# Attention with beacon keys, then an ELU feed-forward, on one core: batch 2's q and k loaded directly and transposed on TensorE, another order of work

## The chip, the core and the metric

The kernel runs on one NeuronCore of a Trainium2 chip. The core has five engines that run side by side and meet at semaphores: TensorE (PE, with its weight loads shown apart as PEld), VectorE (DVE), ScalarE (ACT), GpSimd (POOL) and SyncE (SP). SP, ACT and POOL issue DMAs. The metric is the device time of one execution in microseconds (us), lower is better.

## What is computed

Inputs and output are float32. B = 8 batches, H = 8 heads, S = 576 positions, 16 beacon keys, D = 64; the feed-forward goes from 512 to 2048 and back.

```
scores = (1/8) * q @ concat(beacon_k, k).T      # 576 x 592 for each batch and head
scores = where(causal, -1e9, scores)            # beacon keys are always seen
a      = softmax(scores);  y = a @ concat(beacon_v, v)
x      = y as [B*S, H*D] = [4608, 512]
h      = x @ w_in                               # [4608, 2048]
g      = where(h > 0, h, exp(min(h, 0)) - 1)    # ELU
out    = g @ w_out                              # [4608, 512]
```

## The kernel before

The program is one long list of words, `run("""...""")` near the end. Each word is a call: `F.2.11` is step F with arguments 2 and 11. The words are issued in that order, and each engine takes its own instructions out of them in the same order, so the list sets the order on PE, ACT, DVE, POOL and SP; an engine waits only for its own data, for the buffers that it writes, and for what is ahead of it in its queue.

*Loads of q and k.* `BD` is the number of batches, counted from 0, that are loaded directly. For these `lq.b.n.h0.h1` (L136, two DMAs, q and k, issued by POOL) casts a segment of rows of heads h0 to h1 to bfloat16 in SBUF (`qst`, `kst`; two buffer sets, batch b uses set b % 2). `T.b.p.n` (L267) turns the pair of heads p by transposing matmuls into PSUM; for b > 0 one T is 24 of them, and its PSUM tile is one of the two buffers with the tag "S", which the scores use too. `ck` (ACT) and `cq` (DVE) (both L280) copy the result to the operand tile `qks[p]`, and `cb.b.p` (DVE, L276) puts the beacon keys of that batch beside it. Batch 0 has two segments of rows, batch 1 one. For the batches from `BD` on, `lk.b.n` (L756, POOL) casts q (n = 0) or k (n = 1) from DRAM to a scratch tensor `scr` in DRAM; `lt.b.x` (L763, SP) reads it back by two DMA transposes, one of `scr` for q and one for k, into `qst` (x = 0, head pairs 0 and 1) or `kst` (x = 1, pairs 2 and 3); `lp.b.x` (POOL) fills in the beacon keys.

*Other loads, all by POOL:* `lv` (v, L144 and L149, one DMA for the beacon rows and one for each chunk of keys), `wi` (w_in, L161, eight DMAs each), `wo` (w_out, L165, one each). POOL keeps eight DMAs under way: an issue waits for the eighth before it to land.

*Attention.* `S.b.i` (L321): scores of a group of columns into an S buffer. `x.b.i` (ACT, L336): exp of it into `et`. `m` (DVE, L341): causal masks. The denominators: for batches below `BD`, `L.b.g` sums over all five chunks of keys by matmuls with ones (L378); from `BD` on, `D.b.p.n` (DVE, L394) adds the chunks up first and L does one matmul per head on the sum (L420). `n` (ACT): its reciprocal, by Ln and Exp. `W` (L378): the product with v. `M` (DVE): scaling into x transposed, `xT`.

*Feed-forward.* Tokens go in tiles t of 512 (tiles 0 and 1 have 256). `F.t.i` (L512): one part of h into a PSUM bank of the tag "hps". ELU has two ways: `e` (ACT, exp), `u` (ACT, relu), `k` (DVE, min of exp - 1 and relu: L537); or `e` (ACT), `r` (DVE, L544: min(exp, 1) - 1), `g` (DVE, L550: max with h). Tiles 8 and 9 have P, K, E, U, V instead of F, e, u, k, a form with seven products in place of eight; U is on ACT, or with `.v` on DVE (L724). `G` and `o`, `s` are the output product of the tiles 0 and 1 and its storing. `wt`, `Z`, `Q`, `J` do the same for the later tiles in the form with seven products; `J` copies or adds a result, on ACT or (`.v`) on DVE. `H` and `X` prepare the sums for P. `Jh.9.0` (copy on ACT, DMA on SP) and `Jh.9.1` (copy on DVE, DMA on ACT; L743, L745) store the last two pieces. `warm` and `wm` are matmuls on zeros whose results nobody reads.

The form of r before, and the step that L takes by batch:

```
nc.vector.scalar_tensor_tensor(
    out=rb[t, i], in0=eb[t, i], scalar=1.0, in1=one32.to_broadcast([P, 512]),
    op0=ALU.min, op1=ALU.subtract)
...
if b >= BD:
    for i in range(4):
        nc.tensor.matmul(
            out=r_[32 * i:32 * (i + 1), QA:S], lhsT=ones,
            rhs=presum[b, 2 * g + i // 2][:, i % 2, QA:S], start=True, stop=True, skip_group_check=True)
else:
    quad(b, g, QA, S, r_[:, QA:S], None, True)
```

Of the kernel before, what the change touches and what calls it, by code (L numbers as in the profile page):

```python
# [17 lines left out]
def kernel(  # L18
# [59 lines left out]
    BD = 2  # L78
# [462 lines left out]
    @step  # L541
    def r(t, i):
        rb[t, i] = melt.tile([P, 512], FP16, tag="r", name="r")
        nc.vector.scalar_tensor_tensor(  # L544
            out=rb[t, i], in0=eb[t, i], scalar=1.0, in1=one32.to_broadcast([P, 512]),
            op0=ALU.min, op1=ALU.subtract)
# [391 lines left out]
```

## Time and profile before

| | |
|---|---|
| median of 3 runs | 339.74 us (339.73 to 340.63) |
| span of the profiled execution | 340.2 us, 8575 instructions |
| mean granted TensorE clock | 0.982 |
| PE's longest wait | 4.39 us, up to 57.04 us |
| PE's last matmul ends | 336.4 us |
| DMA moved | 35.82 MB; 71.9% of 16 engines' span on the queue of POOL, 25.4% on that of SP |

The profile is of one execution on the chip. PE, DVE and ACT are shown with the time that they were busy; an arrow `<-` after an instruction names what ended the idle time before it. Line numbers (L512) are those of the kernel, names like `hps<-xT,w_in` are the tile written and the tiles read. A timeline line gives the start, the time until the last of its instructions ended, engine, line, operation, tiles and count.

### The profile page before, as it was taken

The numbers are of one execution on the slowest core, as the hardware profiler recorded it, in microseconds if no ns is written. First come the engines' busy times: TensorE is split into PE (matmuls) and PEld (weight loads), VectorE is DVE, ScalarE is ACT, GpSimd is POOL, SyncE is SP. The second block draws the span as 40 slices with busy tenths as digits, with TensorE's granted clock in tenths as the row PEclk, the third lists the DMA queues.
The fourth block names the chain that finished last, engine by engine and source line by source line (L and its number), as shares of the span: only waits on it lengthen the run. The fifth ranks groups of instructions, "written<-read, shape, count | busy, mean of one in ns | idle before, by whom it ended". The sixth has DMA issues, their size and how long they took to land. (4 is left out here: it accounts for less than half of the span.)

```text
span 340.2 us, 8575 instructions
## 1 busy us (share of the span) xinstructions
PE 324.1 (95%) x3475; PEld 207.2 (61%) x3475; DVE 286.0 (84%) x603; ACT 280.4 (82%) x458; POOL 90.0 (26%) x117
## 2 busy tenths in 40 slices
PE   6989794999999999999999999999999999999995
PEld 3756562544345566555666655566566788788784
DVE  2764774399989999798999987999899999999872
ACT  2998693879899999999889899979988679977940
POOL 8968626226405094005250050000000000000000
PEclk9998997899999999999999999999999999999998
DMA  9999999999999999979999449100001110020112
GB/s 118 149 179 159 158 178 134 147 162 137 179 158 161 121 141 158 174 145 162 80 145 132 98 26 119 56 31 33 33 31 34 33 63 33 0 94 33 62 65 93
DMA packets 141497, 35.82 MB, mean 105 GB/s; under 512 B 126865, under 2 KB 139921, under 8 KB 141457
## 3 DMA queue, kind: packets, MB, share of 16 engines
q0 software_dynamic: 102592, 18.49, 71.9%
q1 hardware_dynamic: 38144, 16.52, 25.4%
q8 instruction: 27, 0.44, 0.5%
q10 hardware_dynamic: 720, 0.26, 0.3%
q14 instruction: 14, 0.11, 0.1%
HBM read 37.22 MB, written 16.52 MB: 158 GB/s over the span
## 5 line engine op out<-in xcount | busy, mean ns | idle before, releaser
L512 PE MATMUL hps<-xT,w_in 128*128 128x512 f16 (+1 forms) x544 | 120.7, 359 | 1.6 <-DVE gt L550 1.3
L336 ACT ACTIVATE et<-sc 128x1024 f16<-128x1024 f32 (+2 forms) x114 | 105.7, 977 | 9.8 <-PE sc L321 9.5
L623 PEld LDWEIGHTS <-gt 128*128 128x128 f16 x768 | 74.1, 98 | 18.7 <-issue 1.7
L522 ACT ACTIVATE e<-hps 128x512 f32<-128x512 f32 x120 | 73.4, 620 | 13.8 <-PE hps L512 9.2
L512 PEld LDWEIGHTS <-w_in 128*128 128x128 f16 x544 | 50.9, 99 | 45.5 <-issue 8.3
L537 DVE SCALAR_TENSOR_TENSOR gt<-e,r 128x512 f16<-128x512 f32 x108 | 72.5, 684 | 6.1 <-ACT e L522 5.2
L527 ACT ACTIVATE r<-hps 128x512 f16<-128x512 f32 x108 | 65.9, 620 | 3.0 <-PE hps L512 2.9
L623 PE MATMUL ops<-wt,gt 128*128 128x256 f16 x384 | 51.1, 273 | 0.0
L623 PE MATMUL ops<-w_out,gt 128*128 128x256 f16 x384 | 48.9, 273 | 0.0
L149 POOL DMA_DIRECT2D v<-in_v_dram x40 | 35.2, 933 | 17.3 <-DMA scr<-in_k_dram 5.8
L580 DVE TENSOR_TENSOR gt<-gt 128x1024 f16<-128x1024 f16 x48 | 32.3, 685 | 0.3
L341 DVE TENSOR_TENSOR et<-et,triu 128x512 f16<-128x512 f16 (+4 forms) x108 | 31.3, 332 | 1.5 <-ACT et L336 1.5
L394 DVE TENSOR_TENSOR qk<-qk,et 128x672 f16<-128x672 f16 (+2 forms) x72 | 26.0, 370 | 1.0
L378 PEld LDWEIGHTS <-v 128*32 128x32 f16 (+1 forms) x800 | 17.3, 96 | 11.0 <-issue 3.1
L378 PE MATMUL ut<-et,v 128*32 128x464 f16 (+3 forms) x560 | 20.7, 296 | 0.1
L639 DVE TENSOR_TENSOR osb<-ops,sm 128x512 f32<-128x512 f32 x24 | 16.4, 684 | 4.4 <-issue 3.3
L321 PE MATMUL sc<-qst 64*128 64x336 bf16 (+11 forms) x192 | 15.1, 260 | 5.2 <-DMA qst<-scr 4.7
L472 DVE TENSOR_TENSOR xT<-ut,rl 128x672 f16<-128x672 f32 (+12 forms) x26 | 16.5, 671 | 3.2 <-ACT rl L438 1.8
L394 DVE TENSOR_TENSOR qk<-et 128x928 f16<-128x928 f16 x24 | 15.2, 636 | 2.3 <-PE lt L420 1.1
L559 PE MATMUL ops<-w_out,gt 128*128 128x512 f16 x64 | 16.8, 394 | 0.0
L732 DVE SCALAR_TENSOR_TENSOR gt<-e,r 128x512 f16<-128x512 f32 x24 | 15.8, 686 | 1.1 <-ACT e L715 0.8
L623 PE MATMUL ops<-w_out,s 128*128 128x256 f16 x128 | 16.6, 273 | 0.0
(109 smaller groups left out, 383.1 us busy)
## 6 DMA issues: line engine op xcount, KB each, us to landing
out_dram<-osb SPq DMA_DIRECT2D x35, 256.0 KB, 2.3
scr<-in_q_dram POOLq DMA_DIRECT2D x6, 576.0 KB, 14.1
scr<-in_k_dram POOLq DMA_DIRECT2D x6, 576.0 KB, 15.4
v<-in_v_dram POOLq DMA_DIRECT2D x24, 128.0 KB, 7.7
w_in<-in_moe_w_in_dram POOLq DMA_DIRECT2D x16, 128.0 KB, 5.5
w_out<-in_moe_w_out_dram POOLq DMA_DIRECT2D x4, 512.0 KB, 18.1
v<-in_v_dram POOLq DMA_DIRECT2D x8, 112.0 KB, 7.1
v<-in_v_dram POOLq DMA_DIRECT2D x8, 80.0 KB, 8.2
```

Source lines behind the costliest of these rows:

```text
L149: nc.gpsimd.dma_start(out=vt[b][r0:r0 + n, j, :, :], in_=v[b, :, ilo[j]:ilo[j] + n, :].rearrange("h s d -> s h d"),)
L336: nc.scalar.activation(out=ets[b, d][:, :, a - EC2 * d:e - EC2 * d], in_=sc[b, g][:, :, a - c0:e - c0], func=AFT.Exp, bias=0.0, scale=SCALE)
L341: nc.vector.tensor_tensor(out=o, in0=o, in1=i, op=ALU.mult)
L378: nc.tensor.matmul(out=t[32 * i:32 * (i + 1), a - qa:e - qa], lhsT=ones[0:kc[j], :] if half is None else v16[0:kc[j], j, h, 32 * half:32 * ...
L394: (nc.vector if eng == "v" else nc.gpsimd).tensor_tensor(out=o, in0=t[0:rows, :, a:e] if n == 0 else o, in1=t[0:rows, :, col:col + e - a], ...
L512: nc.tensor.matmul(out=h[:, n_, :], lhsT=w_in16[:, cc, P * fc:P * (fc + 1)], rhs=xt[k][:, cc, a - TT * k:e - TT * k], start=(cc == 0), sto ...
L522: nc.scalar.activation(out=eb[t, i], in_=flat(hp[t, i]), func=AFT.Exp, bias=0.0, scale=1.0)
L527: nc.scalar.activation(out=rb[t, i], in_=flat(hp[t, i]), func=AFT.Relu, bias=0.0, scale=1.0)
L537: nc.vector.scalar_tensor_tensor(out=half(t, i), in0=eb[t, i], scalar=1.0, in1=rb[t, i], op0=ALU.subtract, op1=ALU.min)
L559: nc.tensor.matmul(out=ob[t, tb_], lhsT=gt[:, fc, P * tb_:P * (tb_ + 1)], rhs=w_out16[:, fc, :], start=(fc == 0), stop=(fc == NFC - 1))
L580: (nc.vector if eng == "v" else nc.gpsimd).tensor_tensor(out=o_, in0=a_, in1=b_, op=op_)
L623: nc.tensor.matmul(out=xy[t, n_][:, qd, :], lhsT=lw[:, P * qd:P * (qd + 1)], rhs=wt_[:, c, :], start=(first and qd == 0 and c == 0), stop= ...
```

## The change

`BD` becomes 3, so batch 2 takes the way of batches 0 and 1: `lq.2.0.0.4` and `lq.2.0.4.8` in place of `lk.2.*`, `lp.2.*` and `lt.2.*`; four words `T.2`, two `cq.2` and two `ck.2`, four `cb.2`; and no `D.2`, as L sums batch 2 over all chunks on PE. Step r takes another instruction for t of 6 and more. All words are put in another order. In it `wo.0` and `wo.1` stand around batch 2's loads and `wo.2`, `wo.3` behind them, ahead of the casts `lk.3.*`. Twenty parts of h take the way over r and g (twelve before; the six with t of 6 or more use the new r), seven U words are on DVE (four before), and eleven J copies are on DVE (fifteen before, the other four now on ACT). There are 72 `wm` matmuls in place of 59. `Jh.9.1` stands before `Jh.9.0`.

```diff
-    BD = 2
+    BD = 3
...
-        nc.vector.scalar_tensor_tensor(
-            out=rb[t, i], in0=eb[t, i], scalar=1.0, in1=one32.to_broadcast([P, 512]),
-            op0=ALU.min, op1=ALU.subtract)
+        if t < 6:
+            nc.vector.scalar_tensor_tensor(
+                out=rb[t, i], in0=eb[t, i], scalar=1.0, in1=one32.to_broadcast([P, 512]),
+                op0=ALU.min, op1=ALU.subtract)
+        else:
+            nc.vector.tensor_scalar(
+                out=rb[t, i], in0=eb[t, i], scalar1=1.0, scalar2=1.0, op0=ALU.min, op1=ALU.subtract)
...
-    S.1.1 x.1.1 S.1.2 m.0.1.2 H.1.1 x.1.2 lk.2.0 cb.1.2 F.0.2 e.0.2 cb.1.1 S.1.5 x.1.5 F.0.1
-    e.0.1 L.0.B n.0.B lk.2.1 r.0.2 S.1.0 wo.0 g.0.2 r.0.1 g.0.1 F.0.0 wo.1 F.0.3 x.1.0 u.0.3
...
-    x.1.11 e.1.4 r.1.4 S.1.9 wo.2 x.1.6 e.0.6 S.1.7 g.1.4 x.1.7 r.0.6 g.0.6 m.1.0.0 F.1.5 e.1.5
...
-    e.1.2 F.1.0 wo.3 k.1.2 S.1.10 x.1.10 G.0.1.0 G.0.0.0 H.1.2 m.1.1.0 m.1.2.1 m.1.2.0 S.2.3
-    x.2.3 F.0.7 e.0.7 S.2.0 S.2.1 lk.3.0 x.2.1 m.1.3.1 m.1.3.0 x.2.0 G.0.1.1 H.2.2 m.1.0.1 L.1.1
...
+    S.1.8 F.1.5 k.0.4 H.1.0 e.0.6 r.0.6 x.1.8 wo.0 lq.2.0.4.8 g.0.6 G.0.1.0 e.1.5 r.1.5 g.1.5
+    S.1.12 x.1.12 lq.2.0.0.4 wo.1 S.1.9 x.1.9 F.1.2 lv.1.0.1 S.1.10 x.1.10 F.1.3 m.1.2.1 cb.2.1
+    wo.2 e.1.3 T.2.2.0 u.1.3 cq.2.2.0 T.2.1.0 ck.2.1.0 G.0.0.0 e.1.2 u.1.2 T.2.0.0 lv.1.2.3.4
+    ck.2.0.0 lv.2.2.3.4 T.2.3.0 k.1.3 wo.3 cq.2.3.0 F.0.7 G.0.0.1 cb.2.0 e.0.7 m.1.0.0 m.1.2.0
+    S.2.1 x.2.1 wt.1.0 S.2.0 m.1.1.0 G.0.1.1 F.1.0 m.1.0.1 S.2.3 lp.4.0 x.2.0 m.1.1.1 m.2.0.0
+    m.1.3.1 u.0.7 L.1.0 m.1.3.0 e.1.0 r.1.0 g.1.0 x.2.3 F.1.6 n.1.0 M.1.0.0 k.0.7 L.1.1 H.1.2
+    n.1.1 G.0.1.2 lk.3.0 e.1.6 u.1.6 M.1.1.0 lv.2.0.1 k.1.2 W.1.0 M.1.0.1 W.1.1 S.2.2 M.1.1.1
...
-    Q.9.98.105 Q.9.105.112 J.9.5 Jh.9.0 Jh.9.1
+    Q.9.42.49 Q.9.49.56 Q.9.56.63 J.9.2.v Q.9.63.70 Z.9.4.0 J.9.3.v Q.9.70.77 Z.9.4.1 Q.9.77.84
+    Q.9.84.91 J.9.4 Q.9.91.98 Q.9.98.105 J.9.5 Q.9.105.112 Jh.9.1 Jh.9.0
```

More of the change, by code (lines that the diff above doesn't have):

```diff
@@ new lines @@
+    wm.4 x.0.1.1 T.0.2.1 S.0.3.0 wm.4 wm.4 x.0.3.0 T.0.3.1 cq.0.2.1 cq.0.3.1 S.0.2.0 wi.0
+    S.0.2.3 x.0.2.0 wm.4 wm.4 x.0.2.3 wm.4 wm.4 m.0.0.0 m.0.2.0 m.0.1.0 S.0.3.1 x.0.3.1 wm.4
+    S.0.1.2 x.0.1.2 m.0.3.0 cb.1.3 L.0.A S.0.0.3 S.0.2.1 x.0.0.3 x.0.2.1 wm.4 S.0.3.2 x.0.3.2
+    T.1.0.0 n.0.A T.1.1.0 wm.4 wm.4 W.0.A.0 cb.1.0 cq.1.0.0 m.0.2.3 S.1.1 m.0.1.3 m.0.1.2
+    m.0.3.2 cb.1.1 ck.1.1.0 x.1.1 wm.4 wm.4 S.1.2 W.0.A.1 x.1.2 S.0.3.3 x.0.3.3 S.0.2.2 m.0.0.3
+    x.0.2.2 M.0.A.0 M.0.A.1 F.0.2 e.0.2 u.0.2 k.0.2 lv.0.3.4 S.1.5 x.1.5 m.0.2.2 S.1.0 F.0.1
@@ new lines @@
+    m.4.0.1 u.4.3 J.2.6.v S.4.6 S.4.5 Z.3.3.1 m.4.1.0 Q.3.0.7 x.4.5 k.4.3 x.4.6 F.4.7 e.4.7
+    Q.3.7.14 u.4.7 m.4.0.0 F.4.6 S.5.4 e.4.6 u.4.6 m.4.1.1 x.5.4 S.4.7 k.4.8 Q.3.14.21 Z.3.1.1
+    D.4.0.0 Z.3.2.1 J.3.0 lv.5 x.4.7 Q.3.21.28 F.4.9 e.4.9 Z.3.2.0 Q.3.28.35 Z.3.4.0 u.4.9
+    m.4.2.0 k.4.7 k.4.9 S.4.9 x.4.9 S.5.2 x.5.2 F.4.2 D.4.0.1 lk.6.0 J.3.1 e.4.2 r.4.2 F.4.1
+    e.4.1 u.4.1 S.5.3 S.5.0 k.4.6 x.5.0 x.5.3 Q.3.35.42 g.4.2 Q.3.42.49 F.4.5 e.4.5 u.4.5
+    m.4.3.0 D.4.1.0 D.4.1.1 F.4.4 e.4.4 S.4.8 S.5.1 Q.3.49.56 lk.6.1 u.4.4 J.3.2.v lt.6.0
@@ new lines @@
+    D.5.0.0 Q.3.98.105 x.5.12 x.5.7 F.5.6 lp.6.0 S.6.1 e.5.6 k.4.1 x.6.1 lk.7.1 u.5.6 lt.6.1
+    m.5.1.0 Q.4.0.7 Q.3.105.112 Z.4.3.0 D.5.1.0 m.5.1.1 S.6.4 x.6.4 D.5.0.1 S.5.9 x.5.9 k.5.6
+    D.5.0.2 D.5.1.1 J.3.6 k.4.13 Q.4.7.14 F.4.11 e.4.11 u.4.11 F.5.7 Z.4.1.0 Z.4.2.0 S.5.11
+    x.5.11 e.5.7 k.4.11 S.5.8 D.5.1.2 D.5.1.3 lt.7.0 Q.4.14.21 m.5.3.1 x.5.8 F.5.11 e.5.11
+    m.5.2.0 u.5.7 D.5.0.3 Q.4.21.28 W.5.0 J.4.0.v Z.4.1.1 u.5.11 L.5.0 n.5.0 lp.7.0 F.5.14
+    k.5.11 Q.4.28.35 m.5.2.1 F.5.1 Z.4.2.1 H.4.1 D.5.2.0 k.5.7 Q.4.35.42 M.5.0.0 J.4.1 e.5.14
@@ new lines @@
+    x.6.10 S.6.0 F.5.3 Q.4.84.91 k.5.9 F.6.4 x.6.0 e.5.3 k.5.0 D.6.1.0 m.6.0.0 e.6.4 k.5.4
+    D.6.0.0 m.6.0.1 S.6.6 S.6.8 x.6.8 x.6.6 Q.4.91.98 Q.4.98.105 Q.4.105.112 J.4.5 D.6.0.1
+    S.6.11 u.5.3 m.6.2.1 k.5.3 Q.5.0.7 J.4.6.v F.6.11 Q.5.7.14 m.6.1.1 u.6.4 k.6.4 F.6.6 x.6.11
+    S.6.12 e.6.11 r.6.11 S.7.2 Z.5.3.0 Z.5.1.0 Q.5.14.21 e.6.6 g.6.11 Z.5.1.1 u.6.6 x.7.2
+    J.5.0.v Z.5.2.0 Z.5.2.1 D.6.0.2 D.6.1.1 F.6.5 lv.6 x.6.12 F.6.15 e.6.5 u.6.5 S.7.4 x.7.4
+    D.6.0.3 S.6.7 m.6.3.0 Q.5.21.28 Q.5.28.35 e.6.15 D.6.1.2 D.6.1.3 r.6.15 k.6.5 J.5.1 x.6.7
@@ new lines @@
+    Q.6.28.35 m.7.3.1 k.7.10 e.7.13 F.7.1 D.7.1.3 u.7.13 m.7.2.0 D.7.0.3 Z.6.2.1 L.7.0 e.7.1
+    S.7.8 s.1.1 u.7.1 m.7.3.0 D.7.3.0 J.6.1 n.7.0 D.7.3.1 k.7.7 k.7.13 M.7.0.0 Q.6.35.42 H.3.0
+    x.7.8 Z.6.4.1 F.7.4 e.7.4 u.7.4 k.7.4 D.7.2.0 F.7.8 e.7.8 k.7.1 u.7.8 D.7.3.2 m.7.2.1
+    D.7.3.3 k.7.8 Q.6.42.49 Q.6.49.56 F.7.5 e.7.5 u.7.5 Z.6.4.0 H.3.1 F.7.14 e.7.14 D.7.2.1
+    J.6.2 D.7.2.2 Q.6.56.63 r.7.14 F.7.6 e.7.6 u.7.6 Q.6.63.70 J.6.3 Q.6.70.77 k.7.6 F.7.9 W.7.0
+    e.7.9 D.7.2.3 L.7.1 n.7.1 Z.7.3.0 k.7.5 r.7.9 g.7.14 g.7.9 Q.6.77.84 F.7.11 J.6.4 X.8.1
@@ new lines @@
+    E.8.1.6 U.8.1.6 K.8.1.5 J.7.1 Q.7.35.42 E.8.1.5 P.8.2.0 K.8.2.0 Q.7.42.49 J.7.2 P.8.2.1
+    U.8.1.4.v V.8.1.4 Z.7.4.0 K.8.2.1 V.8.1.6 Z.7.4.1 Q.7.49.56 P.8.2.2 K.8.2.2 P.8.2.3
+    Q.7.56.63 X.9.1 K.8.2.3 U.8.2.1 E.8.2.1 U.8.1.5.v P.8.2.4 K.8.2.4 Q.7.63.70 J.7.3 V.8.2.1
+    P.8.2.5 P.8.2.6 V.8.1.5 Q.7.70.77 K.8.2.5 Z.8.3.0 E.8.2.6 Q.7.77.84 J.7.4 F.8.13 Z.8.1.0
+    U.8.2.4 U.8.2.6 V.8.2.6 E.8.2.4 V.8.2.4 M.7.1.1 e.8.13 u.8.13 F.8.15 e.8.15 k.8.13 u.8.15
+    k.8.15 Q.7.84.91 F.8.14 e.8.14 F.8.12 u.8.14 k.8.14 e.8.12 Q.7.91.98 J.7.5 u.8.12 Q.7.98.105
@@ new lines @@
+    k.8.12 P.9.0.0 E.8.2.5 K.9.0.0 U.8.2.5 X.9.2 P.9.0.1 Q.7.105.112 P.9.0.2 K.9.0.1 P.9.0.3
+    E.9.0.1 V.8.2.5 K.9.0.2 Q.8.0.7 X.9.3 Z.8.3.1 K.9.0.3 U.9.0.1 X.9.4 P.9.0.4 K.9.0.4 P.9.0.5
+    K.9.0.5 J.7.6 U.9.0.5 Q.8.7.14 P.9.0.6 E.9.0.6 Q.8.14.21 V.9.0.1 P.9.1.0 Z.8.2.0 U.9.0.6
+    U.9.0.4.v K.9.1.0 Z.8.1.1 E.9.0.4 Q.8.21.28 P.9.1.1 P.9.1.2 J.8.0 Q.8.28.35 Z.8.2.1
+    Q.8.35.42 E.9.0.5 K.9.1.1 P.9.1.3 V.9.0.6 V.9.0.4 K.9.1.2 E.9.1.1 P.9.1.4 J.8.1 V.9.0.5
+    K.9.1.3 K.9.1.4 U.9.1.1 Q.8.42.49 J.8.2 P.9.1.5 Q.8.49.56 E.9.1.4 U.9.1.4 K.9.1.5 U.9.1.5
@@ new lines @@
+    V.9.1.1 V.9.1.4 Z.8.4.1 Z.8.4.0 P.9.1.6 E.9.1.6 U.9.1.6 V.9.1.6 F.9.12 e.9.12 Q.8.56.63
+    u.9.12 Q.8.63.70 k.9.12 E.9.1.5 V.9.1.5 P.9.2.0 K.9.2.0 J.8.3 P.9.2.1 K.9.2.1 E.9.2.1
+    U.9.2.1.v Q.8.70.77 P.9.2.2 K.9.2.2 Q.8.77.84 P.9.2.3 J.8.4 K.9.2.3 Q.8.84.91 V.9.2.1
+    P.9.2.4 Z.9.3.0 Q.8.91.98 K.9.2.4 J.8.5 P.9.2.5 P.9.2.6 K.9.2.5 U.9.2.4 E.9.2.4 Q.9.0.7
+    E.9.2.6 U.9.2.6.v V.9.2.4 V.9.2.6 E.9.2.5 U.9.2.5.v F.9.13 e.9.13 u.9.13 Z.9.1.0 V.9.2.5
+    F.9.14 k.9.13 e.9.14 u.9.14 Q.8.98.105 k.9.14 F.9.15 e.9.15 u.9.15 Z.9.3.1 Q.8.105.112 J.8.6
@@ L909 @@
+    Q.9.7.14 Q.9.14.21 k.9.15 Q.9.21.28 Z.9.2.0 Z.9.1.1 J.9.0 Z.9.2.1 Q.9.28.35 Q.9.35.42 J.9.1
+    Q.9.42.49 Q.9.49.56 Q.9.56.63 J.9.2.v Q.9.63.70 Z.9.4.0 J.9.3.v Q.9.70.77 Z.9.4.1 Q.9.77.84
+    Q.9.84.91 J.9.4 Q.9.91.98 Q.9.98.105 J.9.5 Q.9.105.112 Jh.9.1 Jh.9.0
     """)
```

179 lines of the change are left out of this document (63 added, 116 removed).

## The prediction

> **What bounds the kernel now.** I read the page's busy shares first, then the busy time by windows, then PE's waits, then PE's timeline at the longest of them and the two DMA queues behind it.
>
> ```profile
> PE 324.1 (95%) x3475; PEld 207.2 (61%) x3475; DVE 286.0 (84%) x603; ACT 280.4 (82%) x458; POOL 90.0 (26%) x117
> ```
>
> ```profile
> 24.00:28.00 4.00, 3.71 (x25) 1.80 (x25) 2.71 (x12) 3.22 (x5) 2.35 (x6) 0.57 1.30 158
> ...
> 57.00:62.00 5.00, 4.96 (x24) 1.91 (x24) 1.38 (x2) 3.15 (x4) 1.97 (x3) 0.51 1.72 136
> ...
> 66.00:90.00 24.00, 23.97 (x228) 10.77 (x216) 22.44 (x44) 21.07 (x35) 11.33 (x13) 1.00 2.15 161
> 90.00:140.00 50.00, 49.43 (x532) 27.77 (x532) 47.30 (x105) 47.29 (x76) 17.70 (x17) 1.00 1.78 148
> ```
>
> Columns: the window, its length, busy us and instructions of PE, PEld, DVE, ACT and POOL, the granted clock, DMA share, GB/s. From 66 us PE is busy nearly without a gap to its last matmul at 336.4 us, so whatever PE loses or has to do before or after then comes out at the end one for one. It loses most before 66 us: two stretches at half clock, and these waits:
>
> ```profile
> PE sc L321 <- DMA qst<-scr: 4.7, 2, 4.4
> ...
> PE tp L267 <- DMA kst<-in_k_dram: 1.0, 1, 1.0
> ```
>
> ```profile
> 40.44 0.45 PE L267 MATMUL tp<-identb,qst 96*64 96x96 bf16 x12
> 40.72 0.42 PE L267 MATMUL tp<-identb,kst 96*64 96x96 bf16 x12
> 41.07 0.39 PE L321 MATMUL sc<-hi 64*128 64x400 bf16 x4
> ...
> 57.04 0.61 PE L321 MATMUL sc<-qst 64*128 64x48 bf16 x6 [4.39 <-DMA qst<-scr]
> 57.58 1.89 PE L512 MATMUL hps<-xT,w_in 128*128 128x256 f16 x8
> ...
> 62.09 0.90 PE L378 MATMUL lt<-et,ones 128*32 128x464 f16 x24
> ...
> 62.92 0.89 PE L378 MATMUL lt<-et,ones 128*32 128x464 f16 x24
> ...
> 87.79 0.38 PE L420 MATMUL lt<-qk,ones 128*32 128x464 f16 x4
> ...
> 88.25 1.90 PE L559 MATMUL ops<-w_out,gt 128*128 128x512 f16 x8
> ```
>
> ```profile
> 29.83 2.23 POOL L756 DMA_DIRECT2D scr<-in_q_dram  x1
> 31.53 2.76 POOL L756 DMA_DIRECT2D scr<-in_k_dram  x1
> ```
>
> ```profile
> 41.48 6.97 SPq L763 DMA_TRANSPOSE qst<-scr  x2
> 48.57 8.94 SPq L763 DMA_TRANSPOSE kst<-scr  x2
> ```
>
> This is batch 2's way: POOL issues the casts to DRAM at 29.83 and 31.53, they land at 41.4 and 45.1, SP's transposes start only then, and the second lands at 57.0, where the first scores of batch 2 (S.2.3) start after 4.39 us of nothing. The clock is then 0.51 until 62 us.
>
> **The change, part by part** (against the profiled execution's span of 340.2 us; the runs' median, 339.74, lies 0.46 lower).
>
> (1) *The stall.* Four direct loads of 288 KB replace casts and transposes. Wi.1, the last transfer ahead of both, landed at 33.1. Behind it now come 576 KB of batch 1's q and k, 512 KB of w_out, then 1152 KB for batch 2. The queue's rate: from 33.1 to 45.1 before, 1728 KB landed (144 KB/us); from 45.1 to 78.0, 3792 KB and 1152 KB of transposes (150 KB/us). At 150 the loads are complete at 33.1 + 2240/150 = 48.0 us. PE reaches T.2 by its own work: F.0.2 starts at 24.8 before, and 23 us of PE words (each priced by its row) stand between it and T.2.2.0 in the new order; with the 2 to 3 us of small waits that this stretch has now, 50 us. So the data is ahead and the 4.4 us go: -4.4 (bounds -4.4 and 0).
>
> (2) *The half clock behind it.* F.0.7 took 1.82 us from 57.58 to 59.40, against 0.87 for such a word at full clock, G.0.1.1 1.72 against 0.87, the three score words 0.5 more together: 2.3 us lost. Without the long idle stretch it goes: -2.3. [...]
>
> (3) *New PE work.* Each T.2 is 24 transposes like those at 40.44: 0.63 us to the next word (41.07), four times, 2.5. Batch 2's denominators are summed by PE over all key chunks (L.2 as L.1): 62.09 to 62.92, 0.83 us, in place of 87.79 to 88.25, 0.46; twice 0.37, 0.74. These lie in the bound stretch: +3.3. Thirteen more filler matmuls (some 0.06 us each) stand before 24 us, where ACT is the busy engine (11.3 of 12 us from 8 to 20) and PE would wait for its exponentials: 0, or 0.7 if that cover is gone.
>
> (4) *Drains of T.2.* They are a new link: each T.2 takes one of the two S buffers until a copy of 1.36 us on DVE (two) or 1.10 on ACT (two, rows of batch 1's L280) frees it; queued behind them on ACT are the e and u of F.1.2 and F.1.3, whose banks PE needs. Hidden wholly they cost 0, bare all four 4.9. G.0.0.0 and F.0.7 (0.87 each) lie between and after, and e.1.2 and e.1.3 stand ahead of both ACT copies: nearer to hidden, I take +1.0.
>
> (5) *T.1.3's wait for kst, 0.99 us.* That load took 9.0 us with the two casts behind it; batch 1's first halves took 6.4 and 7.1. At 7 it would land at 36.2, ahead of PE: -0.7 (bounds -1.0 and +1.0).
>
> (6) *DVE and ACT.* They fall out of the bound but not far.
>
> ```profile
> L394 DVE TENSOR_TENSOR qk<-qk,et 128x672 f16<-128x672 f16 (+2 forms) x72 | 26.0, 370 | 1.0
> ...
> L394 DVE TENSOR_TENSOR qk<-et 128x928 f16<-128x928 f16 x24 | 15.2, 636 | 2.3 <-PE lt L420 1.1
> ```
>
> ```profile
> L544 DVE SCALAR_TENSOR_TENSOR r<-e,one 128x512 f16<-128x512 f32 x12 | 8.3, 690 | 6.8 <-ACT e L522 6.6
> ...
> L724 DVE TENSOR_SCALAR r<-kst 128x512 f16<-128x512 f32 x2 | 0.8, 422 | 0.0
> ```
>
> DVE loses batch 2's sixteen presums, (26.0 + 15.2)/6 = 6.9, and four sum copies (2.7); it gains two T.2 copies (2.7), four beacon copies (0.6), one copy of batch 0 (0.8), three U words (1.3), and eight tiles that swap u and k for r and g: 8 x 0.69 for each of r, g and minus k is 5.5, less six r's (t of 6 and 7) at the two-scalar form. That form is not in the trace; the nearest row is L724, one scalar at 0.42; bounds 0.42 and L544's 0.69, so six of them save 0 to 1.6, I take 1.6. Sum -0.3: DVE stays at 286. ACT loses eight relus and three U (6.8) and gains two copies of T.2 and four sum copies (2.2 + 2.4) less one of batch 0 (0.7). Neither is a term, PE's work covers them; bare, they would be worth these 0.3 and 2.9 us, and DVE, at 22.4 of 24 us before 90, is the closer one. POOL loses two casts and two lp's and gains four issues of 0.7.
>
> [...]
>
> (7) *The wait for batch 3.* S.3.3 needs lt.3.0, which needs both casts of batch 3. Behind 33.1 the queue now carries 576 + 2048 (w_out) + 1152 + 592 + 592 (v of 1 and 2) + 1152 = 6112 KB to the second cast: at 150, 73.8 us (78.0 before). The transpose took 10.8 us from there (78.09 to 88.84), so 84.6. PE gets to S.3.3 at: F.0.7 at 57.6 - 4.4 - 0.7 + 2.5 + 1.0 - 1.2 (F.1.0 and S.2.3 now come later), 54.8, plus 29.4 of work and 0.6 of small waits, 84.8. A tie: +0.3 (bounds 0 and 6.2, the second below).
>
> (8) *Order elsewhere.* Words are the same in kind after batch 3, and PE is saturated there: 0, bounds -1.5 (the half clock at 24 to 28 us, which the later fillers might prevent: F.0.2 took 1.94 us to the next word for 0.97) and +2.
>
> (9) *The tail.* Jh.9.1 now precedes Jh.9.0: the last copy on ACT stands behind an ACT DMA that waits for DVE's copy. Before: copy 0.37, copy 0.42, issue 0.37. Now copy 0.42, issue 0.37, copy 0.37, issue 0.34: +0.4 (0 if ACT's order did not matter).
>
> Sum: -4.4 - 2.3 + 3.3 + 1.0 - 0.7 + 0.3 + 0.4 = -2.4, a span of 337.8; less 0.46, **337.3 us**.
>
> **Rivals.** *More is freed*: drains hidden (-1.0), the early half clock gone too (-1.5), no tail (-0.4): 334.4. For it: ACT and DVE have 1.7 to 3.5 idle us in each 10 from 20 to 40. Against: ACT has 9.4 of 10 from 40 to 50.
>
> *The loads come late*: v's loads behind w_out landed some 20 us after issue (38.45 to 59.98). Issued at 31 to 33, batch 2's would land at 53, 3 us after PE wants them: 340.3. Against: that queue held two casts and shared the engines with transposes.
>
> *Slower, the stall moves to S.3.3*: if the queue keeps only the 115 KB/us that its own transfers had from 45.1 to 78.0, or if POOL issues the casts no earlier, the second cast lands at 78.0 or later, lt.3.0 at 88.8, PE waits 4.0 us there and then runs at half clock (2.3): 337.3 - 0.3 + 6.3 = 343.3. It decides from a landing of the second cast after 74 us. For it: the tie in (7). Against: no transposes share the engines from 33 us to the first cast's landing.
>
> *The two-scalar form is not faster*: 1.6 us more on DVE at the end, hidden by PE (39.9 of 40 us from 260 to 300, DVE 39.4): between 0 and 1.6, 338.
>
> **How the numbers follow.** Forecast 0.50, with the slower form of r in it; more freed 0.13; loads late 0.14; stall at S.3.3 0.23. The forecast's own range is 335.5 to 339. No change is within 0.3% (1.0 us). The forecast gives 0.48 faster and 0.02 same, more freed 0.13 faster, loads late 0.02 faster, 0.09 same and 0.03 slower, the stall 0.02 same and 0.21 slower (a short one would be same): faster 0.63, same 0.13, slower 0.24. The range 333.8 to 342.5 leaves out the ends of the first and last rivals.
>
> **What would show it.** No PE wait on qst at the first S.2; T.2 at 50 us; granted clock 1.00 from 50 to 66; F.0.7 at 55; S.3.3 at 85 with a wait under 1 us; PE busy 324 to 326 us; R of t = 6 at 0.42; the last output from SP. It is wrong if PE waits at T.2 for its loads, if S.3.3 waits for over 2 us, or if DVE or ACT opens gaps in PE after 60 us.

## The result, and the profile after

| | before | after |
|---|---|---|
| median | 339.74 us (338.31 to 340.63, 4 runs) | 336.53 us (335.02 to 336.74, 4 runs) |
| ratio to before, 95% interval | | 0.9882, 0.9836 to 0.9927 |
| span of the profiled execution | 340.2 us | 335.0 us |
| mean granted TensorE clock there | 0.982 | 0.993 |
| F.0.2 starts on PE | 24.80 us | 27.88 us |
| F.0.7 starts on PE | 57.58 us | 53.22 us |
| S.3.3 starts on PE | 90.08 us | 83.67 us |
| PE's idle time from F.0.2 to its last matmul | 8.16 us | 0.83 us |
| PE's last matmul ends | 336.42 us | 330.58 us |

The forecast was 337.3 us. By the ratio the change is worth 4.0 us (2.5 to 5.6); by the medians in the table 3.2; by the two profiles 5.2. The time of a run is 1.7 us longer than the span of the same execution (336.74 and 335.0 us for the profiled one of after), so the span of 340.2 us in the profile of before belongs to a time of 341.9 us, 2.2 above the median of before, while the profile of after is 0.2 above its own: the comparison of profiles flatters the change by 2.0 us. The granted clock of that execution of before, 0.982, is as low as that of any other (0.982 to 0.998).

The busy shares of the kernel after, and its PE waits, longest first (total, times, longest us):

```profile
PE 325.6 (97%) x3616; PEld 210.7 (63%) x3616; DVE 284.7 (85%) x601; ACT 278.1 (83%) x452; POOL 90.9 (27%) x117
```

```profile
PE w L207 <- DVE lo L174: 1.3, 1, 1.3
PE tq L267 <- DMA kst<-in_k_dram: 0.9, 1, 0.9
PE tq L267 <- DMA qst<-in_q_dram: 0.6, 1, 0.6
```

The 4.4 us for the transposed scratch are gone, and no wait over 0.4 us is left behind 15 us. Two waits of 0.9 and 0.6 us are new: `tq` is a T of batch 0, so they lie in the head. PE's timeline where the stall was (start, us, engine, line, operation, tiles):

```profile
49.92 0.45 PE L267 MATMUL tp<-identb,qst 96*64 96x96 bf16 x12
50.20 0.42 PE L267 MATMUL tp<-identb,kst 96*64 96x96 bf16 x12
50.45 0.42 PE L267 MATMUL tp<-identb,qst 96*64 96x96 bf16 x12
50.71 0.42 PE L267 MATMUL tp<-identb,kst 96*64 96x96 bf16 x12
51.06 1.04 PE L563 MATMUL ops<-w_out,gt 128*128 128x512 f16 x4
52.07 0.45 PE L267 MATMUL tp<-identb,qst 96*64 96x96 bf16 x12
...
53.22 1.05 PE L512 MATMUL hps<-xT,w_in 128*128 128x256 f16 x8
54.10 1.03 PE L563 MATMUL ops<-w_out,gt 128*128 128x512 f16 x4
55.06 0.61 PE L321 MATMUL sc<-qk 64*128 64x64 bf16 x6
```

T.2.2 starts at 49.92, F.0.7 at 53.22, S.2.1 at 55.06, and no line carries an idle time in brackets. The four T.2 with G.0.0.0 among them fill 3.30 us without a gap, so their drains into SBUF are hidden. The stages (window, length, busy us and instructions of PE, PEld, DVE, ACT, POOL, granted clock, DMA share, GB/s):

```profile
8.00:20.00 12.00, 10.35 (x182) 7.31 (x180) 7.76 (x25) 7.75 (x10) 9.28 (x17) 0.86 1.47 166
24.00:28.00 4.00, 3.64 (x94) 2.52 (x89) 3.63 (x12) 4.00 (x5) 3.52 (x7) 1.00 1.19 159
57.00:62.00 5.00, 5.00 (x99) 2.85 (x101) 4.27 (x12) 4.81 (x9) 5.00 (x7) 1.00 2.34 155
66.00:90.00 24.00, 24.00 (x214) 10.83 (x211) 17.85 (x39) 23.14 (x37) 2.88 (x3) 1.00 1.78 163
90.00:140.00 50.00, 50.00 (x526) 28.88 (x524) 47.01 (x102) 47.18 (x78) 24.01 (x24) 1.00 1.50 122
```

The clock is 1.00 from 57 to 62 us, and PE has no gap at all from 66 to 140. Half clock has moved to the head: 0.86 from 8 to 20 us, with ACT busy for 7.75 us there. The same window of before:

```profile
8.00:20.00 12.00, 11.96 (x264) 8.36 (x260) 7.83 (x28) 11.30 (x16) 9.42 (x18) 1.00 1.44 155
```

Batch 3's transposes on SP's queue, and PE at S.3.3:

```profile
62.73 7.82 SPq L767 DMA_TRANSPOSE qst<-scr  x2
72.26 7.45 SPq L767 DMA_TRANSPOSE kst<-scr  x2
```

```profile
82.74 0.90 PE L378 MATMUL lt<-et,ones 128*32 128x464 f16 x24
...
83.67 0.40 PE L321 MATMUL sc<-qst 64*128 64x48 bf16 x6
```

The second cast landed at 69.1 us and the two transposes into `qst`, which S.3.3 reads, by 77.0; PE came 6.7 us later and did not wait.

**Where 5.2 us went, profile against profile.** PE's end moved by 5.84 us: from the start to F.0.2 3.08 lost, from F.0.2 to F.0.7 7.45 won (32.78 to 25.33), from there to S.3.3 2.05 won (32.50 to 30.45), and behind it 0.58 lost (246.34 to 246.91 to its last matmul). The last store lost 0.68 (3.77 us from PE's end to the span's end, now 4.45). Words cross these marks, so a stretch is no pure measure of a part; the experiments come closer to one.

### The profile page after: what moved, and what is told of

Its sections match the earlier page's. It is cut to its first block, busy times and chain, and to the rows that moved or that the text cites. A ratio compares the mean times of both kernels' runs of the same rounds, so it can differ in the third digit from the quotient of the medians.

```text
span 335.0 us, 8848 instructions
## 1 busy us (share of the span) xinstructions
PE 325.6 (97%) x3616; PEld 210.7 (63%) x3616; DVE 284.7 (85%) x601; ACT 278.1 (83%) x452; POOL 90.9 (27%) x117
## 4 chain that ended last, share of the span: by engine, by line
PE 87%; DVE 3%; ACT 3%; POOL 2%; DMA 2%; issue 1%; ACTq 0%; DVEq 0%; POOLq 0%
PE hps L512 30%; PE ops L627 29%; PE sc L321 8%; PE ut L378 6%; PE hps L697 5%; PE ops L563 4%; PE lt L378 2%; DMA kst<-in_k_dram 2%; ACT et L336 2%; POOL qst L136 1%; PE lt L420 1%; PE w L214 1%; PE tp L267 1%; PE ub L378 1%; DVE gt L554 1%
## 5 line engine op out<-in xcount | busy, mean ns | idle before, releaser
L512 PE MATMUL hps<-xT,w_in 128*128 128x512 f16 (+1 forms) x544 | 118.5, 354 | 0.3
L627 PEld LDWEIGHTS <-gt 128*128 128x128 f16 x768 | 73.3, 98 | 20.2 <-issue 3.7
L537 DVE SCALAR_TENSOR_TENSOR gt<-e,r 128x512 f16<-128x512 f32 x100 | 67.0, 684 | 8.0 <-ACT r L527 7.9
L527 ACT ACTIVATE r<-hps 128x512 f16<-128x512 f32 x100 | 61.9, 626 | 0.0
L627 PE MATMUL ops<-w_out,gt 128*128 128x256 f16 x384 | 50.7, 273 | 0.4 <-DVE gt L537 0.4
L394 DVE TENSOR_TENSOR qk<-qk,et 128x672 f16<-128x672 f16 (+2 forms) x60 | 21.2, 368 | 0.4
L563 PE MATMUL ops<-w_out,gt 128*128 128x512 f16 x64 | 16.0, 380 | 0.0
L736 DVE SCALAR_TENSOR_TENSOR gt<-e,r 128x512 f16<-128x512 f32 x24 | 15.9, 684 | 0.1
L627 PEld LDWEIGHTS <-s 128*128 128x128 f16 x128 | 12.3, 98 | 3.1 <-issue 0.3
L554 DVE TENSOR_TENSOR gt<-hps,r 128x512 f16<-128x512 f32 x20 | 13.7, 687 | 0.7
```

The costliest lines, as they stand in the source:

```text
L512: nc.tensor.matmul(out=h[:, n_, :], lhsT=w_in16[:, cc, P * fc:P * (fc + 1)], rhs=xt[k][:, cc, a - TT * k:e - TT * k], start=(cc == 0), sto ...
L527: nc.scalar.activation(out=rb[t, i], in_=flat(hp[t, i]), func=AFT.Relu, bias=0.0, scale=1.0)
L537: nc.vector.scalar_tensor_tensor(out=half(t, i), in0=eb[t, i], scalar=1.0, in1=rb[t, i], op0=ALU.subtract, op1=ALU.min)
L563: nc.tensor.matmul(out=ob[t, tb_], lhsT=gt[:, fc, P * tb_:P * (tb_ + 1)], rhs=w_out16[:, fc, :], start=(fc == 0), stop=(fc == NFC - 1))
L627: nc.tensor.matmul(out=xy[t, n_][:, qd, :], lhsT=lw[:, P * qd:P * (qd + 1)], rhs=wt_[:, c, :], start=(first and qd == 0 and c == 0), stop= ...
```

## The experiments

The theory: the direct loads take the stall away, but PE reaches that place no sooner unless the new order also closes PE's small waits ahead of it; the two parts need one another. And the head lost 3 us for a reason of its own. The rivals: the direct loads do all of it; the order does all of it; the new r does it.

| run | median us | ratio to before, 95% interval |
|---|---|---|
| after | 336.53 | 0.9882 (0.9836 to 0.9927) |
| direct loads alone | 340.44 | 1.0014 (0.9981 to 1.0047) |
| order with casts and presums | 352.11 | 1.0371 (1.0315 to 1.0427) |
| order with casts, sums on PE | 342.87 | 1.0054 (1.0015 to 1.0094) |
| after, head of before | 334.24 | 0.9824 (0.9782 to 0.9867) |
| after, lv.0.2 later | 334.05 | 0.9820 (0.9781 to 0.9858) |
| after, four tiles of h back on r and g | 339.38 | 0.9988 (0.9954 to 1.0023) |
| after, old r everywhere | 336.71 | 0.9910 (0.9876 to 0.9943) |
| after, two-scalar r everywhere | 335.60 | 0.9889 (0.9847 to 0.9930) |
| lv.0.2 later, Jh.9.0 first | 333.55 | 0.9831 (0.9793 to 0.9869) |
| the same, two-scalar r everywhere | 333.37 | 0.9770 (0.9740 to 0.9801) |

**1. The direct loads alone.** The kernel before with `BD` = 3, in its own order.

```diff
-    BD = 2
+    BD = 3
...
-    lk.2.0
+    lq.2.0.0.4
...
-    lk.2.1
+    lq.2.0.4.8
...
-    x.1.10 G.0.1.0
+    x.1.10 cb.2.0 cb.2.1 T.2.0.0 ck.2.0.0 T.2.1.0 cq.2.1.0 G.0.1.0
+    cb.2.2 cb.2.3 T.2.2.0 ck.2.2.0 T.2.3.0 cq.2.3.0
```

`lp.2`, `lt.2` and `D.2` are taken out.

> The earlier kernel and order with batch 2's direct loads alone (the casts' places hold the loads, T.2 and its copies stand behind the last scores of batch 1, no presums for batch 2). Theory: the terms of the prediction hold without the new order: -4.4 and -2.3 for stall and half clock, +3.3 for PE's new work, +0.5 for drains, span 337 against 340.2. Rival: the direct loads need the new order, and PE waits at T.2's drains, for v of batch 1 (landed at 65.5 us, used at 65.7) or at S.3.3: span 339 to 342.

Measured: 340.44 us, no difference from before. The two profiles do differ, 338.2 and 340.2 us, but the runs of before that were measured beside this one have a median span of 338.3. PE's timeline of this run, where T.2 now stands:

```profile
49.68 0.45 PE L267 MATMUL tp<-identb,qst 96*64 96x96 bf16 x12 [0.53 <-ACT et L336]
49.93 0.45 PE L267 MATMUL tp<-identb,kst 96*64 96x96 bf16 x12
51.09 0.45 PE L267 MATMUL tp<-identb,qst 96*64 96x96 bf16 x12 [0.71 <-ACT et L336]
...
54.84 0.40 PE L321 MATMUL sc<-qk 64*128 64x48 bf16 x6
55.17 1.05 PE L512 MATMUL hps<-xT,w_in 128*128 128x256 f16 x8
```

The stall is gone and the clock stays full there (0.999 over the whole span), yet F.0.7 starts at 55.17, 2.4 us sooner than before, where T.2 has cost its own 2.5 us and 1.24 for S buffers that ACT's exponentials still held. PE's other small waits are all there: 1.36 us for g (DVE, L550) between F.0.2 and F.0.7. From F.0.2 on PE needs 309.07 us, before 311.62, after 302.70, each in its profile. The drains that the prediction priced at 1.0 us are real in this order and nothing in the new one. No other place for T.2 in the old order was tried; it could save these 1.24 us of waits, too little to come near after.

**2 and 3. The order without the direct loads.** First with everything of batch 2's old way:

```diff
-    BD = 3
+    BD = 2
...
-    wo.0 lq.2.0.4.8 g.0.6
+    wo.0 lk.2.0 lk.2.1 lp.2.0 lp.2.1 g.0.6
...
-    x.1.12 lq.2.0.0.4 wo.1 S.1.9
+    x.1.12 wo.1 lt.2.0 lt.2.1 S.1.9
...
-    e.2.13 L.2.0
+    e.2.13 D.2.0.0 D.2.0.1 D.2.0.2 D.2.0.3 D.2.1.0 D.2.1.1 D.2.1.2 D.2.1.3 L.2.0
```

The words T.2, cq.2, ck.2 and cb.2 are taken out, and the other eight D.2 stand ahead of L.2.1.

> The changed kernel's order with batch 2 back on casts and DMA transposes (casts in the place of the first direct load, presums ahead of L.2, no T.2). Theory: the stall comes back: casts land at 43 and 47 us, transposes 10 to 12 us later at 56 to 58, PE wants S.2.1 at 52.5: 4 to 5 us of waiting and 2 of half clock, less 3.3 us of PE work: span 338 to 340. Rival: the new order alone carries the gain and hides the transposes: span 336 or less.

Measured: 352.11 us, 12 more than expected. PE waits 5.63 us for `qst<-scr` at S.2.1, but also 7.2 us in all at the two L.2 for the presums, which I had put directly ahead of them. So this run mixes two costs, and the next one takes the second away: the denominators of batch 2 are summed by PE, as after.

```diff
-            if b >= BD:
+            if b >= 3:
                 for i in range(4):
...
-    e.2.13 D.2.0.0 D.2.0.1 D.2.0.2 D.2.0.3 D.2.1.0 D.2.1.1 D.2.1.2 D.2.1.3 L.2.0
+    e.2.13 L.2.0
```

> The order after, with batch 2's q and k by casts and DMA transposes as before, and batch 2's denominators summed over all chunks by PE as after (no presums D.2). Against the changed kernel only the loads differ, with the four T.2. If the transposes' lateness is what the direct loads take away, S.2.1 again waits some 5.6 us for them and half clock follows for some 2.3, less T.2's 2.5: a span of 340 to 341, a time near 342. If 7.2 us of the 352.1 us of the order with casts were the presums' place, this run comes out at 343 to 345 at most. If the order alone is worse without the direct loads for another reason (the loads of batch 3, GpSimd's queue), it stays near 350, with waits at S.3.3 or later.

Measured: 342.87 us, 0.5% slower than before. Its PE timeline at the stall:

```profile
48.41 1.03 PE L512 MATMUL hps<-xT,w_in 128*128 128x256 f16 x8 [0.46 <-ACT r L527]
49.28 1.03 PE L563 MATMUL ops<-w_out,gt 128*128 128x512 f16 x4
57.62 1.04 PE L321 MATMUL sc<-qst 64*128 64x64 bf16 x6 [7.32 <-DMA qst<-scr]
58.59 1.89 PE L563 MATMUL ops<-w_out,gt 128*128 128x512 f16 x4
60.28 1.91 PE L512 MATMUL hps<-xT,w_in 128*128 128x256 f16 x8
```

From F.0.2 to F.0.7 PE needs 23.43 us with 0.88 idle, 0.46 of it directly ahead of F.0.7 (before: 32.78 with 6.9). The casts were issued at 28.42 and 30.12 us, no later than before (29.83 and 31.53). But the transposes into `qst` are not done before 57.5, so what PE gained ahead of them it waits there: 7.32 us in place of 4.39, and the clock is at half for 10.2 us in place of 6.8, which makes a product of 1.04 us last 1.89. Neither part gains by itself (+0.1% and +0.5%); together they gain 1.2%. That is what the theory said, and it excludes both "one part does all" rivals. Of the +0.5%, some 0.9 us (0.3%) is not the order but PE's work for batch 2's sums, which this run keeps (an estimate: an L.2 by PE took 0.93 us after, one on presums 0.46 before).

**4 and 5. The head.** In the new order `lv.0.2` (two DMAs, 144 KB) is issued ahead of the second half of batch 0's heads. First the whole head of before, then that one word moved.

```diff
-    warm.4 warm.4 lq.0.0.0.4 lq.0.1.0.4 lv.0.2 warm.4 wm.4 ident T.0.0.0 bt
+    lq.0.0.0.4 warm.12 lq.0.1.0.4 lq.0.0.4.8 ident bt bk cb.0.1 cb.0.0
...
-    m.0.0.3 x.0.2.2 M.0.A.0 M.0.A.1 F.0.2
+    m.0.1.2 H.1.1 x.1.2 cb.1.2 cb.1.1 F.0.2
```

> The changed kernel with the earlier kernel's words up to the first F.0.2 (less batch 2's casts and fills) and its own words from there on. Theory: the new order lost 3.1 us ahead of F.0.2 (27.88 against 24.80 us) and everything behind it follows F.0.2, so F.0.2 comes back to 25 us, PE's last matmul from 330.6 to 327.5, the span from 335.0 to about 332. Rival: what follows is held by the DMA queue (the second half of w_in landed at 32.5, batch 2's loads at 44.9) or by ACT, so that PE waits there instead and the span stays at 334 to 335.

```diff
-    warm.4 warm.4 lq.0.0.0.4 lq.0.1.0.4 lv.0.2 warm.4 wm.4
+    warm.4 warm.4 lq.0.0.0.4 lq.0.1.0.4 warm.4 wm.4
...
-    S.0.1.0 x.0.1.0 lv.0.0.1
+    S.0.1.0 x.0.1.0 lv.0.2 lv.0.0.1
```

> The changed kernel with the load of v (lv.0.2) moved from ahead of batch 0's heads 4 to 7 to behind batch 1's first loads, nothing else. Theory: the 144 KB of v ahead made those heads land at 13.5 and 14.8 us (11.4 and 12.3 in the earlier kernel), and PE's waits of 0.6 and 0.9 us for them, the 1.8 us that ACT stood still, and the half clock from 16.3 us come from that: F.0.2 1.5 to 2.5 us earlier, span 333. Rival: the order of the exponentials and the fillers at the head set F.0.2, not the load: span within 0.5 us of 335.0.

Measured: 334.24 and 334.05 us; the one word's place gains as much as the whole head. The profiled execution of run 4 is the longest of its seven (336.01 us, a span of 334.3; the others 333.80 to 334.57): F.0.2 is back at 24.86 us there, but half clock from 24.79 to 28.20 makes PE need 26.83 us to F.0.7, where after needs 25.33. PE's timeline of the kernel after, in the head:

```profile
13.56 0.33 PE L267 MATMUL tq<-identb,qst 80*64 80x80 bf16 x8 [0.60 <-DMA qst<-in_q_dram]
14.82 0.33 PE L267 MATMUL tq<-identb,kst 80*64 80x80 bf16 x8 [0.93 <-DMA kst<-in_k_dram]
...
17.16 1.89 PE L214 MATMUL w<-lo 128*128 128x128 bf16 x16
```

The last rows of heads 4 to 7 landed at 13.51 and 14.78 us (11.44 and 12.27 before), the scores behind them came late for ACT, and 3.4 us of half clock followed: the 16 fillers at 17.16 take 1.89 us (8 of them took 0.62 at 15.38, at full clock) and stand ahead of scores. With `lv.0.2` moved, the window of that run from 8 to 20 us reads

```profile
8.00:20.00 12.00, 11.27 (x230) 8.06 (x230) 7.91 (x27) 10.28 (x14) 8.83 (x16) 1.00 1.53 168
```

with the full clock, and F.0.2 starts at 25.18. How much the early `lv.0.2` costs differs by execution: six profiles with the very same words up to F.0.2 had it at 25.0 and 25.5 (no half clock; the runs of `BD` = 2 with sums on PE and of the old r), 27.9, 27.9, 28.1 and 29.1 us. What differs between them is when the last k of heads 4 to 7 landed: at 13.17 and 13.66 us in the two without half clock, at 14.64 to 14.95 in the other four. In the three profiles with `lv.0.2` later it landed at 11.97 to 13.37, and none has half clock in the head (granted clock 0.998 to 0.999 over their spans).

**6. The two ways of ELU ahead of F.0.7.** In the new order four parts of tile 0, which had r and g, have u and k. Put back:

```diff
-    u.0.1 u.0.2 u.0.4 u.0.5 k.0.1 k.0.2 k.0.4 k.0.5
+    r.0.1 g.0.1 r.0.2 g.0.2 r.0.4 g.0.4 r.0.5 g.0.5
```

(r and g stand where u stood; the lists of words are shortened to the ones exchanged.)

> The changed kernel with four parts of tile 0 (F.0.1, F.0.2, F.0.4, F.0.5) back on r and g, as the earlier kernel has them, r and g in the place of u. Theory: between the first F.0.2 and F.0.7 the earlier kernel's PE waits 1.4 us for g to free its bank and the changed one 0.3, because tile 0 is freed by a relu on ACT; with r and g back PE waits there for g again, 1 to 1.5 us, span 336 to 336.5 against 335.0. Rival: the waits come from the rest of the order (where masks and copies stand on DVE), and the swap changes less than 0.5 us.

Measured: 339.38 us, 2.85 more than after and more than I had expected. PE's waits from 25 to 60 us in this run:

```profile
PE hps L512 <- DVE gt L554: 2.8, 4, 1.0
```

The same wait before, from F.0.2 on:

```profile
PE hps L512 <- DVE gt L550: 1.3, 3, 0.6
```

After has 0.26 us of them between F.0.2 and F.0.7. With u, ACT's relu is the last reader of the bank, so PE gets it back without DVE; with g, PE waits until DVE has done r and g, 0.69 us each and behind masks. From F.0.2 to F.0.7 this run needs 28.03 us, after 25.33: the 2.7 us are nearly the whole difference of the medians (between the profiles, 339.0 and 335.0, the head takes another 1.25). Nor is it the head that makes the medians differ: measured on the same chip, the runs with a clock of 0.997 or more took 336.80 to 337.70 us here and 334.18 to 335.52 with after's u and k (runs 7 and 8). This exchange, which the prediction counted only as DVE and ACT time, is the largest single part of the order's gain that I could isolate.

**7 and 8. The form of r.** `if t < 6` made `t < 10` (the old r in all tiles) and `t < 0` (the two-scalar r in all).

```diff
-        if t < 6:
+        if t < 10:
```

> The changed kernel with r in its old instruction in all tiles. Theory: the six r's of tiles 6 and 7 take 0.69 in place of 0.42 us, and PE's own work hides all 1.6 us of it: span 335.0, ratio to the changed kernel within 0.3%. Rival: DVE is late for PE there, and up to 1.6 us come out at the end, 336.6.

```diff
-        if t < 6:
+        if t < 0:
```

> The changed kernel with the two-scalar r in all tiles, so that fourteen more of them run while GpSimd issues DMAs. Theory: 0.27 us less for each on DVE, hidden by PE, and no time that GpSimd loses can be told: span 335.0. [...]

Measured: 336.71 and 335.60 us; both agree with 336.53 within what the heads of their executions differ by. The trace resolves the first: from L.4.0 to P.8.0.0 PE needs 110.77 us with the old r, 110.11 with the new one, with a wait of 0.39 us for g at 260.25 that after doesn't have. So the new r in the last tiles is worth 0.7 us in the profile, less than the medians resolve; PE's work hides 0.9 of the 1.6 us; I had expected all of it to be hidden. The rival that the new r does it all is out: without it the ratio to before is 0.9910. The row of after has the form's price:

```profile
L545 DVE SCALAR_TENSOR_TENSOR r<-e,one 128x512 f16<-128x512 f32 x14 | 9.6, 688 | 2.6 <-ACT e L522 2.4
...
L549 DVE TENSOR_SCALAR r<-e 128x512 f16<-128x512 f32 x6 | 2.5, 420 | 1.4 <-ACT e L522 1.4
```

**9 and 10. A better version.** `lv.0.2` moved as in run 5, and the last two words exchanged; then also the two-scalar r in all tiles.

```diff
-    J.9.5 Q.9.105.112 Jh.9.1 Jh.9.0
+    J.9.5 Q.9.105.112 Jh.9.0 Jh.9.1
```

> The changed kernel with lv.0.2 behind batch 1's first loads and the last two stores in their old order (Jh.9.0 ahead of Jh.9.1). Theory: the first edit alone gave 334.05 us, and the store order costs 0.5 to 0.65 us (4.4 us from PE's last matmul to the end, 3.8 before): 333.4, and 3.8 us of tail. Rival: the tail is set by the DMA's landing and stays at 4.4: 334.05.

> The changed kernel with lv.0.2 put back, Jh.9.0 first and the two-scalar r in all tiles. If the two-scalar r saves PE's small waits for g before F.0.7 (0.42 to 0.12 us in the run that had it everywhere), it gains 0.2 to 0.3 us: 333.3 us. If VectorE's waits for GpSimd (one r of 1.53 us) reach PE, it is 333.6 or more. Either is within 0.3% of the version without it, 333.55.

Measured: 333.55 and 333.37 us, 1.7% and 2.3% under before by ratios whose base was measured with each (339.60 and 340.85 us); their medians differ by less than 0.3%. The end of the kernel after, and of run 9:

```profile
330.62 0.42 DVE L747 COPY osb<-ops 128x256 f32<-128x256 f32 x1 [1.05 <-PE ops L627]
331.08 0.38 ACTq L749 DMA_DIRECT2D out_dram<-osb  x1
331.57 0.37 ACT L747 COPY osb<-ops 128x256 f32<-128x256 f32 x1 [11.01 <-DVE osb L747]
331.97 0.34 SPq L749 DMA_DIRECT2D out_dram<-osb  x1
```

```profile
327.80 0.37 ACT L747 COPY osb<-ops 128x256 f32<-128x256 f32 x1 [10.05 <-PE ops L627]
328.20 0.34 SPq L749 DMA_DIRECT2D out_dram<-osb  x1
328.21 0.42 DVE L747 COPY osb<-ops 128x256 f32<-128x256 f32 x1 [1.46 <-ACT osb L747]
328.66 0.38 ACTq L749 DMA_DIRECT2D out_dram<-osb  x1
```

After, ACT's copy waits behind ACT's DMA, which waits for DVE's copy; the last issue starts 1.39 us behind PE's end. With `Jh.9.0` first it starts 0.90 us behind it (PE ended at 327.76), and the tail is 4.01 us in place of 4.45.

## Why the prediction was right

The direction, the place and the mechanism were right: the stall and its half clock went, T.2 came without waits, PE was the bound again. That the sum came out near was in part luck, since a loss in the head and gains elsewhere, none of them forecast, nearly cancelled. So it was with T.2: forecast at 50 us and found at 49.92, but from an F.0.2 at 27.88 in place of 24.8 and with 22.0 us between in place of 25 to 26. Its steps, against the profiles:

- *The stall, -4.4.* Right: no wait on qst behind 15 us. But it is worth this only in the new order; by itself the direct loading gained nothing by the medians (run 1). The prediction took the terms as independent, and they are not: run 3 shows that the order by itself makes the stall longer.
- *The half clock behind it, -2.3.* Right for the profiled execution: 1.00 from 57 to 62 us. In the median run it is worth less, since other executions of before had higher clocks. The prediction took 0.46 us between profile and median, but set a span against run times; with the 1.7 us between these two measures it is 2.2. That half clock goes with the long idle stretch was its estimate, and too narrow: its own trace has half clock from 24.40 us too, with no wait over 0.67 us in the 3.41 ahead of it.
- *New PE work, +3.3.* T.2 took 3.30 less 0.87 for G.0.0.0, 2.4 (2.5 forecast), and L.2.0, at 82.74 above, 0.93 (0.83 forecast). The fillers cost little as long as the head keeps its clock: F.0.2 then starts at 25.0 to 25.5 us (24.80 before).
- *Drains, +1.0.* Mis-sized: nothing to be seen in the new order, 1.24 us in the old one. The forecast took a mean between hidden and bare; the words between the T.2 were enough to hide them. One of its reasons was misread: e.1.2 stands behind the first of the two copies on ACT, not ahead of both.
- *kst for T.1.3, -0.7.* Gone whole, -1.0: it landed at 35.47 (36.2 forecast), PE came at 39.2.
- *DVE and ACT, no term.* Their busy times came out as forecast (284.7 and 278.1 us; 286 and 277.5). But "no term" was wrong: the exchange of r and g for u and k moves the release of PE's banks from DVE to ACT, and that is worth 2.7 us (run 6). The prediction priced engine time and not the chain through the bank.
- *The wait for batch 3, +0.3.* Mis-sized: not a tie but 6.7 us to spare. The second cast landed at 69.1 (73.8 forecast) and the transposes at 77.0 (84.6). The queue was faster than the 150 KB/us taken: batch 2's loads were complete at 44.87, not 48.0: 2240 KB in the 12.4 us since w_in's last part landed at 32.46, 181 KB/us. The slower rival had the same weak place, its rate.
- *Order elsewhere, 0 within -1.5 and +2.* This step failed, in both directions, and that the two parts nearly cancelled was luck. Against it: the head lost 3.1 us in the profile, some 2 to 2.5 us by the runs (ratios 0.9882 and 0.9820, medians 336.53 and 334.05), at or beyond the bound. The prediction saw PE's fillers there and not that a load had been put ahead of what ACT waits for. For it: the waits for g ahead of F.0.7 (1.42 us, now 0.26), 1.11 us of waits between S.3.3 and P.8.0.0 that are now zero, and the half clock at 24 us.
- *The tail, +0.4.* Right in kind: 0.7 between the profiles, 0.44 by run 9.

So the forecast's -2.4 us (measured -4.0, from -2.5 to -5.6) came from terms of the right sign, too small on balance: a drain that was hidden, a swap of ELU ways taken at nothing, and against these a head whose loss the forecast had not priced. The rival *more is freed*, 334.4 us, has its price in runs 5, 9 and 10, 333.4 to 334.1, where the head is mended. What isn't settled: of the 6.4 us that PE needs less behind F.0.2 after than with the direct loads alone (309.07 and 302.70), 4.25 are waits (5.08 and 0.83); the other 2.1 no run assigns.

## What to carry to other kernels

A stall that stands late in a row of small waits hides them: taking away the stall alone, or the small waits alone, gained nothing here (ratios 1.0014 and 1.0054, together 0.9882), so price both together and look at what PE would do in the freed time. Of two forms of an operation, the one that gave the scarce buffer back sooner, and from the engine that had time, was the better one here (run 6: 336.53 us with u and k, 339.38 with r and g). And a DMA put ahead of others in the first microseconds was paid by what waited for the first data (run 5: 336.53 us with `lv.0.2` early, 334.05 with it later).

## What the runs showed of the hardware

**Half clock without a long idle time.** Busy time and clock of the 3.4 us ahead of a half-clock stretch and of the stretch itself, in the kernel after and in before (columns as in the stages above):

```profile
12.88:16.29 3.41, 1.87 (x48) 1.44 (x46) 1.17 (x2) 1.57 (x3) 2.94 (x6) 1.00 1.30 176
16.29:19.70 3.41, 3.41 (x43) 2.55 (x36) 3.03 (x15) 1.83 (x4) 1.34 (x3) 0.50 1.66 186
```

```profile
20.99:24.40 3.41, 2.10 (x60) 1.42 (x61) 2.58 (x4) 3.18 (x6) 3.02 (x6) 1.00 1.38 188
24.40:27.80 3.40, 3.40 (x23) 1.52 (x20) 2.11 (x12) 2.62 (x4) 1.80 (x4) 0.50 1.24 158
```

PE was busy for 1.9 and 2.1 of 3.4 us, its longest single wait was 0.93 and 0.67 us, and the clock halved all the same. In six profiles (before, after and runs 2, 4, 6 and 8) a half clock begins within the first 25 us, and in all of them PE was busy for 1.85 to 2.10 us of the stretch ahead, with no wait over 1.36.

In the profiles of before and after each stretch of one clock, the last one left out, lasted 3.413 us or a whole multiple of it (before: full for 20.48 us from 3.92 on, half for 3.41, full for 27.31, half for 6.83, full for 276.48; after: full for 10.24 us from 6.05 on, half for 3.41, full for 314.03), so such stretches are compared here on that grid. On it, a stretch with 2.19 us of PE kept the full clock (with the direct loads alone, from 47.71). Nor did half clock follow every stretch with less: one with 2.06 us of PE kept the full clock (before, from 3.92), and so did one with 1.74 in the run with casts and presums. In the long stall of before the clock halved at 55.12, when PE had waited for 2.46 of its 4.39 us. The stretch of before that ends there, then the one of the run with casts and presums:

```profile
51.70:55.12 3.42, 0.95 (x5) 0.22 (x3) 3.30 (x12) 1.00 (x2) 2.97 (x2) 1.00 1.88 107
```

```profile
87.05:90.47 3.42, 1.74 (x9) 0.59 (x6) 1.61 (x3) 2.71 (x5) 0.00 (x0) 1.00 1.51 199
```

So 1.3 to 1.6 us of idle time in 3.41 were followed by half clock six times, where no single wait was longer than 1.36 us: in this kernel a row of short waits could cost half clock as the wait of 4.39 us did.

**A two-scalar r took up to 1.53 us while POOL issued a cast.** DVE and POOL in the run with the two-scalar r in all tiles:

```profile
56.92 2.75 POOL L760 DMA_DIRECT2D scr<-in_k_dram  x1
...
58.40 1.53 DVE L549 TENSOR_SCALAR r<-e 128x512 f16<-128x512 f32 x1
58.62 1.41 POOL L776 MEMSET qst<- 128x96 bf16 x1
58.74 1.43 POOL L777 COPY qst<-bkT 128x32 bf16<-128x32 bf16 x1
```

r takes 1.53 us in place of 0.42 while POOL issues a cast and starts to fill in beacon keys, 0.83 at 145.46 beside another cast, and 0.56 at 43.60; the other 17 of the 20 take 0.41 to 0.43. The old form took 0.68 in the same place in the kernel after, where POOL issued the same cast. The cast's issue itself took 2.75 us here and 2.72 there, so it is r that takes longer here, by 1.11 us, and not the issue. POOL loses a little behind it: its next cast starts 3.27 us after this one, in after 2.93. The cast's issue had begun 1.48 us ahead of r. Why r takes longer then, no run shows. It cost PE nothing here: from F.0.2 on it needs 302.45 us, after 302.70.
